# Attention with two head mixings and a routed expert layer: scores as float32 products of 64-row tiles, the second mixing in two row tiles, the split for the first mixing on GpSimd

## The chip, the cores and the metric

The kernel runs on one core of one Trainium2 chip. A time is device microseconds (us) of one execution of the whole program. Three runs of the kernel before are given; a change is judged against their median.

## What is computed

For each of 8 batches there are 12 heads, 448 queries and keys, and 64 features per head. The reference, cut to what matters here:

```
scores = (q @ k^T) / 8                              # per batch and head: 448 x 448
scores = einsum('bhij,hg->bgij', scores, w_pre)     # first mixing, over heads
attn   = softmax(scores)                            # over the keys j
attn   = einsum('bhij,hg->bgij', attn, w_post)      # second mixing, over heads
x      = attn @ v                                   # rows of 12 * 64 = 768
out    = gate * relu(x @ w1[e]) @ w2[e]             # e: the best of 8 experts for each row
```

All of it is in float32. The expert layer works on 3584 rows of x.

## The kernel before

The attention works in 32 tiles of up to 120 queries (four to a batch: 120, 120, 120 and 88). Within a tile, the head mixing goes by blocks of 10 queries, so that 10 x 12 = 120 (query, head) rows fill the partitions; the last block of a batch has 8 queries. There are 360 blocks.

- `qk` (line 196) computes the scores of one head of a tile. Both operands are kept as a rounded part and a remainder in the format float32r: the 128 contraction rows hold 64 rows of rounded q and 64 rows of its remainder, and two products, with rounded keys (line 203) and with their remainder (line 204), add up in PSUM. ScalarE copies the result to the tile `si` (line 208). The rounded parts are made by `split_k` (lines 96 and 97) and `split_q` (lines 116 and 117), on ScalarE and VectorE; keys and queries are loaded twice, once for each half of the partitions (lines 89 and 109).
- `relayout` (line 215) is a DMA on the queue of SyncE (SP) that turns 10 queries x 12 heads of `si` into a tile `sb` of 120 partitions x 448 keys.
- `split` (lines 223 and 224) makes a rounded part `sh` and a remainder `sl` of `sb`, on VectorE.
- `mix` (from line 227) is the first mixing: three float32r products of 448 columns (lines 231 to 233), the maximum of each row (line 235, VectorE), the exponential with its row sum (line 237, ScalarE), the reciprocal of the sum (lines 239 and 241), and a copy of the second mixing's weights scaled by it, `wp` (line 243, VectorE).
- `post` (from line 247) is the second mixing: four plain float32 products, one per chunk of 112 keys, each with the exponentials of the chunk as the stationary operand and the 120 columns of `wp` as the moving one (line 256). ScalarE copies the result to `pt` (line 258).
- `av` (from line 263) multiplies `pt` by the values, for a pair of heads at a time: eight float32 products in two column tiles of 64 columns (line 271). `rows` (line 289) turns x and adds the routing logits, and `dispatch` (from line 301) writes the token lists of the experts, with an indirect DMA on GpSimd (line 334).

A loop over the blocks (from line 406) hands out this work one step after another, with leads: scores 17 blocks ahead, relayout 5, split 2, the second mixing 3 behind. The code within a step is sorted by a number, but that is not the order in which the engines run it: outside the prologue (line 393) a planner orders the instructions of each engine by when it reckons their operands ready, with this order as the priority. Each engine then runs its own list strictly in order. The values of the next batch are loaded into the single tile `vt` after the last `av` of a batch (line 277), the keys of the next batch during the scores of a batch's last tile (line 210).

After the attention the expert layer follows, from about 1153 us on. It is left as it is, but for one buffer less for its raw weights and an earlier start of the first weight loads.

Of the kernel before, what the change touches and what calls it, by code (L numbers as in the profile page):

```python
# [8 lines left out]
F32 = mybir.dt.float32  # L9
# [5 lines left out]
ALU = mybir.AluOpType  # L15
# [23 lines left out]
def attn_moe_kernel(ctx, tc, qT, kT, v, w_pre, w_post, w_gate, w1, w2, out):  # L39
# [15 lines left out]
    kq = ctx.enter_context(ExitStack())  # L55
    kraw_p = kq.enter_context(tc.tile_pool(name="kraw", bufs=2, side="right"))
    k_p = kq.enter_context(tc.tile_pool(name="kp", bufs=6, side="right"))
    q_p = kq.enter_context(tc.tile_pool(name="qp", bufs=1, side="right"))
    att = ctx.enter_context(ExitStack())
    v_p = att.enter_context(tc.tile_pool(name="vp", bufs=1))  # L60
    si_p = att.enter_context(tc.tile_pool(name="sip", bufs=2))
    sb_p = att.enter_context(tc.tile_pool(name="sbp", bufs=4))
    sh_p = att.enter_context(tc.tile_pool(name="shp", bufs=3))
    e_p = att.enter_context(tc.tile_pool(name="ep", bufs=5))
    sm_p = att.enter_context(tc.tile_pool(name="smp", bufs=4))
    ps_s = att.enter_context(tc.tile_pool(name="ps_s", bufs=1, space=PSUM))
# [5 lines left out]
    bank_s = [ps_s.tile([P, 512], F32, name=f"bs{n}") for n in range(2)]  # L72
    bank_m = [ps_m.tile([IT, 512], F32, name=f"bm{n}") for n in range(2)]
    bank_p = [ps_p.tile([JC, 512], F32, name=f"bp{n}") for n in range(2)]
    bank_a = ps_a.tile([P, 3, IT], F32, name="ba")
    bank_x = [ps_x.tile([P, 512], F32, name="bx"), bank_s[0]]
    turn = {"s": 0, "m": 0, "p": 0}

    def bank(k, banks):
        turn[k] += 1  # L80
        return banks[turn[k] % len(banks)]

    KK, QQ, VV, SI, SB, SH, EE, PT, XT, KR = ({} for _ in range(10))

    def dma_k(b, c, pool):
        raw = pool.tile([P, KC, S], F32, name="kraw")
        src = kT[b, c * KC:(c + 1) * KC].rearrange("h d j -> d h j")
        for half in range(2):
            nc.sync.dma_start(out=raw[half * D:(half + 1) * D], in_=src)
        KR[b, c] = raw  # L90

    def split_k(b, c, eng=None):
        raw = KR.pop((b, c))
        ka = k_p.tile([P, KC, S], F32R, name="ka")
        kb = k_p.tile([P, KC, S], F32R, name="kb")
        nc.scalar.copy(out=ka, in_=raw)
        (eng or nc.vector).tensor_sub(out=kb, in0=raw, in1=ka.bitcast(F32))  # L97
        KK[b, c] = (ka, kb)

    def load_k(b, c):  # L100
        dma_k(b, c, kraw_p)
        split_k(b, c)

    def dma_q(T):
        b, it, ni, _ = geom[T]
        raw = q_p.tile([P, H, IT], F32, name="qraw")
        src = qT[b, :, H * it * IT:H * (it * IT + ni)].rearrange("d (h i) -> d h i", h=H)
        for half in range(2):
            nc.sync.dma_start(out=raw[half * D:(half + 1) * D, :, :ni], in_=src)
        KR[T] = raw  # L110

    def split_q(T):
        b, it, ni, _ = geom[T]
        raw = KR.pop(T)
        qs = q_p.tile([P, H, IT], F32R, name="qs", bufs=2)
        nc.scalar.copy(out=qs[:, :, :ni], in_=raw[:, :, :ni])
        nc.vector.tensor_sub(out=qs[D:P, :, :ni], in0=raw[D:P, :, :ni],
                             in1=qs[D:P, :, :ni].bitcast(F32))
        QQ[T] = qs

    def load_q(T):
        dma_q(T)
        split_q(T)

    def load_v(b):
        vt = v_p.tile([JC, NJ, HD], F32, name="vt")
        nc.sync.dma_start(out=vt, in_=v[b].rearrange("(c p) f -> p c f", p=JC))
        VV[b] = vt

    w12 = const.tile([IT, 2, H], F32, name="w12")  # L130
    for n, w in enumerate((w_pre, w_post)):
        nc.scalar.dma_start(out=w12[:, n, :], in_=w.unsqueeze(0).to_broadcast([IB, H, H]))
# [3 lines left out]
    first = ExitStack()  # L136
    first_p = first.enter_context(tc.tile_pool(name="kfirst", bufs=H // KC))
    dma_q(0)
    for c in range(H // KC):
        dma_k(0, c, first_p)  # L140

# [4 lines left out]
    # mask[p, i] = 1 where p // 12 == i  # L146
    mask = const.tile([IT, IB], F32, name="mask")
    nc.gpsimd.memset(mask, 1.0)
    nc.gpsimd.affine_select(out=mask, in_=mask, pattern=[[-H, IB]], compare_op=ALU.is_ge,
                            fill=0.0, base=0, channel_multiplier=1)  # L150
    nc.gpsimd.affine_select(out=mask, in_=mask, pattern=[[H, IB]], compare_op=ALU.is_ge,
                            fill=0.0, base=H - 1, channel_multiplier=-1)
    Wraw = const.tile([IT, IB, H], F32, name="Wraw")
    WH = const.tile([IT, IT], F32R, name="WH")
    WL = const.tile([IT, IT], F32R, name="WL")
    Wpost = const.tile([IT, H, IB], F32, name="Wpost")
    # SCALE is a power of two: exact
    nc.vector.scalar_tensor_tensor(out=Wraw, in0=w12[:, 0:1, :].to_broadcast([IT, IB, H]),
                                   scalar=SCALE, in1=mask.unsqueeze(2).to_broadcast([IT, IB, H]),
                                   op0=ALU.mult, op1=ALU.mult)  # L160
    nc.vector.tensor_tensor(out=Wpost, in0=w12[:, 1, :].unsqueeze(2).to_broadcast([IT, H, IB]),
                            in1=mask.unsqueeze(1).to_broadcast([IT, H, IB]), op=ALU.mult)
    Wraw = Wraw.rearrange("p i g -> p (i g)")
    nc.vector.tensor_copy(out=WH, in_=Wraw)
    nc.vector.tensor_sub(out=WL, in0=Wraw, in1=WH.bitcast(F32))

    # xg[:, c] = [identity | w_gate of chunk c]: rows of x and partial logits in one product
# [4 lines left out]
    tri = const.tile([P, P], BF16, name="tri")      # tri[m, n] = 1 where m < n  # L172
# [14 lines left out]
    # rows that no token has taken: a token id out of range, gate 0  # L187
# [8 lines left out]
    def qk(T, h):  # L196
        b, it, ni, _ = geom[T]
        if h == 0:
            SI[T] = si_p.tile([IT, H, S], F32, name="si")
        ps = bank("s", bank_s)  # L200
        ka, kb = KK[b, h // KC]
        qs = QQ[T][:, h, :ni]
        nc.tensor.matmul(out=ps[:ni, :S], lhsT=qs, rhs=ka[:, h % KC, :], start=True, stop=False)  # L203
        nc.tensor.matmul(out=ps[:ni, :S], lhsT=qs, rhs=kb[:, h % KC, :], start=False, stop=True)  # L204
        if T == 0 and h % 3 == 2:
            nc.vector.tensor_copy(out=SI[T][:ni, h, :], in_=ps[:ni, :S])
        else:
            nc.scalar.copy(out=SI[T][:ni, h, :], in_=ps[:ni, :S])  # L208
        if it == 3 and b + 1 < B and h % KC == KC - 1:
            load_k(b + 1, h // KC)  # L210

    def relayout(T, s):
        nb = geom[T][3][s]
        sb = sb_p.tile([IT, S], F32, name="sb")
        nc.sync.dma_start(out=sb[:nb * H], in_=SI[T][s * IB:s * IB + nb])
        SB[T, s] = sb

    def split(T, s):
        R = geom[T][3][s] * H
        sb = SB.pop((T, s))  # L220
        sh = sh_p.tile([IT, S], F32R, name="sh")
        sl = sh_p.tile([IT, S], F32R, name="sl")
        nc.vector.tensor_copy(out=sh[:R], in_=sb[:R])  # L223
        nc.vector.tensor_sub(out=sl[:R], in0=sb[:R], in1=sh[:R].bitcast(F32))  # L224
        SH[T, s] = (sh, sl)

    def mix(T, s):
        R = geom[T][3][s] * H
        sh, sl = SH.pop((T, s))
        pm = bank("m", bank_m)  # L230
        nc.tensor.matmul(out=pm[:R, :S], lhsT=WH[:R, :R], rhs=sh[:R], start=True, stop=False)  # L231
        nc.tensor.matmul(out=pm[:R, :S], lhsT=WL[:R, :R], rhs=sh[:R], start=False, stop=False)  # L232
        nc.tensor.matmul(out=pm[:R, :S], lhsT=WH[:R, :R], rhs=sl[:R], start=False, stop=True)  # L233
        st = sm_p.tile([IT, 4], F32, name="st")
        nc.vector.reduce_max(out=st[:R, 0:1], in_=pm[:R, :S], axis=AX.X, negate=True)  # L235
        et = e_p.tile([IT, S], F32, name="et")
# [8 lines left out]
        EE[T, s] = (et, wp)  # L245

    def post(T, s):
        nb = geom[T][3][s]
        R = nb * H
        if s == 0:  # L250
            PT[T] = pt_p.tile([JC, NJ, H, IT], F32, name="pt")
# [420 lines left out]
```

## Time and profile before

| what | value |
|---|---|
| runs | 1745.09, 1730.40, 1741.92 us; median 1741.92 us |
| profiled execution | span 1726.5 us from the first to the last instruction; the page gives no other time of its own |
| busy time of TensorE (matmul) | 1541.7 us, 89% of the span |
| busy time of VectorE, ScalarE, GpSimd | 1055.8, 903.9, 109.3 us |
| mean granted TensorE clock | 0.949 |
| DMA | 219.58 MB, 127 GB/s on average |

A row of the trace gives a start in us from the beginning of the span and a duration. A float32 matmul stands in it as two matmul records, each with a weight load of its own; a float32r matmul is one record. The duration of a matmul record includes the way through the array, so that records overlap: how fast TensorE works is read from the distance between starts. PE is TensorE's matmul, PEld its weight load, DVE is VectorE, ACT is ScalarE, POOL is GpSimd.

### The profile page before, as it was taken

What the parts mean: (1) busy time and instruction counts of PE and PEld (TensorE: products, weight loads), DVE (VectorE), ACT (ScalarE), POOL (GpSimd) and SP (SyncE); (2) the same over time, 40 slices, a digit from 0 to 9 for tenths busy, and PEclk for the clock granted to TensorE, in tenths of its full rate; (3) what the DMA queues carried; (4) which work ended last, traced back from release to release, by engine and by line L of the source; (5) the groups of instructions that cost most, each with busy time, mean ns of one, the idle gap of its engine ahead of it and who ended that gap; (6) DMA issues with size and microseconds to landing.
All of it is one profiled execution on the core that took longest, in us unless ns stands there. A gap on an engine that the chain in (4) does not pass through costs nothing. (4 is left out here: it accounts for less than half of the span.)

```text
span 1726.5 us, 30276 instructions
## 1 busy us (share of the span) xinstructions
PE 1541.7 (89%) x11032; PEld 1341.1 (78%) x11032; DVE 1055.8 (61%) x3159; ACT 903.9 (52%) x1940; POOL 109.3 (6%) x119
## 2 busy tenths in 40 slices
PE   5878978987988988998898898968999999999996
PEld 3667867876876877786787787758898988898986
DVE  4677857876877777786786787753433425335330
ACT  4566756765766656675775676633422314224220
POOL 1000000000000000000000000010110201101000
PEclk9999988999999989998998999988999999999998
DMA  8666656666556666665665655634514326145210
GB/s 180 129 134 129 127 117 137 116 134 140 118 126 148 121 137 128 130 126 129 134 117 128 133 110 114 154 70 162 195 67 165 142 78 215 66 153 210 74 62 34
DMA packets 112169, 219.58 MB, mean 127 GB/s; under 512 B 28226, under 2 KB 83538, under 8 KB 112004
## 3 DMA queue, kind: packets, MB, share of 16 engines
q1 hardware_dynamic: 104896, 193.53, 48.3%
q0 software_dynamic: 6064, 23.86, 3.7%
q8 instruction: 98, 1.61, 0.4%
q14 instruction: 67, 0.55, 0.1%
q10 hardware_dynamic: 1044, 0.04, 0.0%
HBM read 118.03 MB, written 23.06 MB: 82 GB/s over the span
## 5 line engine op out<-in xcount | busy, mean ns | idle before, releaser
L256 PE MATMUL bp<-wp,et 120*112 120x120 f32 (+1 forms) x2880 | 386.1, 276 | 4.2 <-ACT pt L258 2.7
L256 PEld LDWEIGHTS bp<-wp,et 120*112 120x112 f32 (+1 forms) x2880 | 346.7, 180 | 45.4 <-issue 21.4
L258 ACT COPY pt<-bp 112x480 f32<-112x480 f32 x360 | 204.3, 568 | 143.1 <-PE bp L256 142.2
L208 ACT COPY si<-bs 120x448 f32<-120x448 f32 (+1 forms) x380 | 200.8, 531 | 140.4 <-PE bs L204 108.0
L271 PE MATMUL ba<-pt,vt 112*64 112x120 f32 (+1 forms) x3072 | 210.7, 276 | 50.1 <-DMA vt<-in_v 40.7
L237 ACT ACTIVATE et<-bm,st 120x448 f32<-120x448 f32 x360 | 229.5, 638 | 43.2 <-DVE st L235 34.9
L271 PEld LDWEIGHTS ba<-pt,vt 112*64 112x64 f32 x3072 | 162.6, 142 | 110.7 <-issue 95.5
L235 DVE TENSOR_REDUCE st<-bm 120x1 f32<-120x448 f32 x360 | 220.9, 614 | 12.4 <-PE bm L233 12.1
L224 DVE TENSOR_TENSOR sl<-sb,sh 120x448 fp32r<-120x448 f32 x360 | 220.5, 615 | 0.3
L223 DVE CAST sh<-sb 120x448 fp32r<-120x448 f32 x360 | 140.0, 389 | 101.6 <-PE bm L232 51.3
L203 PE MATMUL bs<-ka,qs 128*120 128x448 f32 (+1 forms) x384 | 153.7, 400 | 48.0 <-ACT si L208 33.1
L231 PE MATMUL bm<-sh,WH 120*120 120x448 f32 x360 | 167.6, 465 | 7.6 <-DVE sh L223 4.7
L204 PE MATMUL bs<-kb,qs 128*120 128x448 f32 (+1 forms) x384 | 148.5, 387 | 0.6 <-DVE kb L97 0.6
L500 PE MATMUL pm_h<-xh,ah 128*128 128x512 f32 (+1 forms) x384 | 146.9, 383 | 2.2 <-PEq L552 0.8
L500 PE MATMUL pm_h<-xl,ah 128*128 128x512 f32 (+1 forms) x384 | 146.4, 381 | 0.0
L500 PE MATMUL pm_h<-xh,al 128*128 128x512 f32 (+1 forms) x384 | 146.4, 381 | 0.0
L233 PE MATMUL bm<-sl,WH 120*120 120x448 f32 x360 | 137.6, 382 | 0.2 <-DVE sl L224 0.2
L232 PE MATMUL bm<-sh,WL 120*120 120x448 f32 x360 | 137.5, 382 | 0.0
L519 PE MATMUL pm_y<-bh,hh 128*128 128x384 f32 x480 | 127.9, 343 | 0.0
L504 DVE SCALAR_TENSOR_TENSOR hl<-pm_h,hh 128x512 fp32r<-128x512 f32 (+1 forms) x64 | 42.0, 656 | 136.3 <-ACT hh L503 136.3
L203 PEld LDWEIGHTS bs<-ka,qs 128*120 128x120 f32 (+1 forms) x384 | 72.6, 189 | 67.0 <-ACT si L208 39.9
L519 PE MATMUL pm_y<-bl,hh 128*128 128x384 f32 x480 | 123.6, 336 | 0.0
(106 smaller groups left out, 2177.4 us busy)
## 6 DMA issues: line engine op xcount, KB each, us to landing
sb<-si SPq DMA_DIRECT2D x352, 210.0 KB
wraw<-in_w SPq DMA_DIRECT2D x48, 512.0 KB
wraw<-in_w SPq DMA_DIRECT2D x64, 384.0 KB
kraw<-in_kT SPq DMA_DIRECT2D x96, 224.0 KB
qraw<-in_qT SPq DMA_DIRECT2D x48, 360.0 KB
vt<-in_v SPq DMA_DIRECT2D x8, 1344.0 KB
XD<-xr SPq DMA_DIRECT2D x24, 360.0 KB
qraw<-in_qT SPq DMA_DIRECT2D x16, 264.0 KB
```

What stands on the lines that cost most here:

```text
L203: nc.tensor.matmul(out=ps[:ni, :S], lhsT=qs, rhs=ka[:, h % KC, :], start=True, stop=False)
L204: nc.tensor.matmul(out=ps[:ni, :S], lhsT=qs, rhs=kb[:, h % KC, :], start=False, stop=True)
L208: nc.scalar.copy(out=SI[T][:ni, h, :], in_=ps[:ni, :S])
L224: nc.vector.tensor_sub(out=sl[:R], in0=sb[:R], in1=sh[:R].bitcast(F32))
L231: nc.tensor.matmul(out=pm[:R, :S], lhsT=WH[:R, :R], rhs=sh[:R], start=True, stop=False)
L235: nc.vector.reduce_max(out=st[:R, 0:1], in_=pm[:R, :S], axis=AX.X, negate=True)
L237: nc.scalar.activation(out=et[:R], in_=pm[:R, :S], func=AF.Exp, bias=st[:R, 0:1], scale=1.0, accum_out=st[:R, 1:2])
L256: nc.tensor.matmul(out=ppv[:, c, :], lhsT=et[:R, c * JC:(c + 1) * JC], rhs=wp[:R, :, :nb], start=True, stop=True)
L258: nc.scalar.copy(out=PT[T][:, :, :, s * IB:s * IB + nb].rearrange("p c h i -> p (c h) i"), in_=pp[:, :NJ * R].rearrange("p (x i) -> p x i" ...
L271: nc.tensor.matmul(out=pa[r * D:(r + 1) * D, :ni], lhsT=VV[b][:, c, h * D:(h + 1) * D], rhs=PT[T][:, c, h, :ni], start=(c == 0), stop=(c = ...
L500: nc.tensor.matmul(out=ph[:, :n], lhsT=wx[:, fs], rhs=xx[:, kt, :n], start=(m == 0), stop=(m == 3 * NK1 - 1))
L519: nc.tensor.matmul(out=py[g][:, :384], lhsT=hx[:, kt, ts], rhs=wx[:, g * 384:(g + 1) * 384], start=(n == 0), stop=(n == 3 * NK2 - 1))
```

## The change

- The scores are plain float32 products. A pair of heads lies in one tile of 128 partitions (64 each), and the two heads are multiplied in two row tiles of the array, each over 224 keys at a time, into two PSUM banks. ScalarE copies both banks in one instruction. Keys and queries are no longer split, and are loaded once. There are buffers for the keys of two batches.
- A step now holds two blocks of 10 queries, side by side in the free dimension (`[P, 2, S]`), so there are 184 steps. The 120 rows lie on partitions 4 to 123, so that the first five queries end at partition 64.
- The first mixing keeps its three float32r products per block. The rounded part and the remainder are made by GpSimd, for both blocks in one instruction each, as is the scaled `wp`.
- The second mixing runs in two row tiles: five queries in partitions 4 to 63, five in 64 to 123. Each product has 60 columns in place of 120, and each row tile has a PSUM bank of its own. VectorE copies the results, one instruction per bank.
- The values have two tiles, and those of the next batch are loaded at step 8 of a batch. The leads are, in steps of two blocks: scores 9, relayout 3, split 1; the second mixing is 1 behind.

```
 def qk(T, c):
...
+        for n in range(2):
+            ns = slice(n * S // 2, (n + 1) * S // 2)
+            for r in range(2):
+                hs = slice(r * D, (r + 1) * D)
+                nc.tensor.matmul(out=bank_s[:ni, r, ns], lhsT=qt[hs, c, :ni], rhs=kt[hs, ns],
+                                 start=True, stop=True)
+        nc.scalar.copy(out=SI[T][:ni, 2 * c:2 * c + 2, :], in_=bank_s[:ni, :, :S])
+        if it == 1 and b + 1 < B:
+            load_k(b + 1, c)
...
 def relayout(T, s):
+        sb = sbs[nsb["n"] % len(sbs)]
+        nsb["n"] += 1
+        for c, nq in enumerate(geom[T][3][s]):
+            q0 = s * NB + c * IB
+            nc.sync.dma_start(out=sb[R0:R0 + nq * H, c, :], in_=SI[T][q0:q0 + nq])
...
 def split(T, s):
-        nc.vector.tensor_copy(out=sh[:R], in_=sb[:R])
-        nc.vector.tensor_sub(out=sl[:R], in0=sb[:R], in1=sh[:R].bitcast(F32))
+        sh = sh_p.tile([P, 2, S], F32R, name="sh")
+        sl = sh_p.tile([P, 2, S], F32R, name="sl")
+        nc.gpsimd.tensor_copy(out=sh[:R1, :nh], in_=sb[:R1, :nh])
+        nc.gpsimd.tensor_sub(out=sl[:R1, :nh], in0=sb[:R1, :nh], in1=sh[:R1, :nh].bitcast(F32))
...
 def mix(T, s):
+        for c in range(nh):
+            for n, (w, x) in enumerate(((WH, sh), (WL, sh), (WH, sl))):
+                nc.tensor.matmul(out=bank_m[:R1, c, :S], lhsT=w[:R1, :], rhs=x[:R1, c, :],
+                                 start=(n == 0), stop=(n == 2))
+        nc.vector.reduce_max(out=st[:R1, 0, :nh], in_=bank_m[:R1, :nh, :S], axis=AX.X, negate=True)
+        for c in range(nh):
+            nc.scalar.activation(out=et[:R1, c, :], in_=bank_m[:R1, c, :S], func=AF.Exp,
+                                 bias=st[:R1, 0, c:c + 1], scale=1.0,
+                                 accum_out=st[:R1, 1, c:c + 1])
...
+        wp = e_p.tile([P, 2, WPC], F32, name="wp")
+        for c in range(nh):
+            nc.gpsimd.tensor_scalar(out=wp[:R1, c, :], in0=Wpost[:R1], scalar1=st[:R1, 2, c:c + 1],
+                                    scalar2=None, op0=ALU.mult)
...
 def post(T, s):
+        for n in range(len(halves)):
+            for c in range(NJ):
+
+                for r in range(2):
+                    ps = slice(64 * r, 64 if r == 0 else R1)
+                    x0 = (n * NJ + c) * WPC
+                    nc.tensor.matmul(out=bank_p[r][:, x0:x0 + WPC],
+                                     lhsT=et[ps, n, c * JC:(c + 1) * JC],
+                                     rhs=wp[ps, n, :], start=True, stop=True)
+        for r in range(2):
+            pv = bank_p[r][:, :2 * NJ * WPC].rearrange("p (n x i) -> p n x i", n=2, i=IQ)
+            if len(halves) == 2:
...
+                nc.vector.tensor_copy(out=dst, in_=pv.rearrange("p n x i -> p x n i"))
...
 def av(T, pr):
-        if pr == NPAIR - 1 and it == 3 and b + 1 < B:
-            load_v(b + 1)
...
-    PL, QLEAD, RLEAD, SLEAD = 3, 17, 5, 2
+    PL, QLEAD, RLEAD = 1, 9, 3
...
+            at(max(u0 - QLEAD - 3, -1), 0, load_q, T)
+        if it == 0 and b + 1 < B:
+            at(u0 + 8, 2, load_v, b + 1)
+        for c in range(NPAIR):
+            at(max(u0 - QLEAD + c * 5 // 6, -1), 3, qk, T, c)
         for s in range(n):
             at(max(u0 + s - RLEAD, -1), 4, relayout, T, s)
-            at(max(u0 + s - SLEAD, -1), 5, split, T, s)
+            at(max(u0 + s - 1, -1), 5, split, T, s)
             at(u0 + s, 1, mix, T, s)
             at(u0 + s + PL, 7, post, T, s)
...
-            wpool["raw"] = moe.enter_context(tc.tile_pool(name="wrp", bufs=4, side="right"))
+            wpool["raw"] = moe.enter_context(tc.tile_pool(name="wrp", bufs=3, side="right"))
...
-        if u > ustart[NTILE - 1] and u - ustart[NTILE - 1] <= NK1:
-            load_w(0, w1, u - ustart[NTILE - 1] - 1, FF, "a")
+        if u > ustart[NTILE - 1] - 3 and u - ustart[NTILE - 1] + 3 <= NK1:
+            load_w(0, w1, u - ustart[NTILE - 1] + 2, FF, "a")
```

## Rows read from the trace of the kernel before

**Rows 1.** The page: busy time by engine, and in 40 slices of the span (about 43 us each) TensorE's busy share and the granted clock, in tenths.

```profile
PE 1541.7 (89%) x11032; PEld 1341.1 (78%) x11032; DVE 1055.8 (61%) x3159; ACT 903.9 (52%) x1940; POOL 109.3 (6%) x119
PE   5878978987988988998898898968999999999996
PEclk9999988999999989998998999988999999999998
```

**Rows 2.** Three stretches of the attention at full clock, with TensorE's instructions of line 231 alone, one per block of 10 queries: the stretch, its length, their busy time and count, granted clock, DMA share, GB/s.

```profile
145.00:214.00 69.00, 12.05 (x27) 1.00 0.61 123
...
705.00:775.00 70.00, 12.50 (x28) 1.00 0.60 120
...
985.00:1050.00 65.00, 11.16 (x25) 1.00 0.59 117
```

**Rows 3.** TensorE in order of time: the first product of the first mixing, and the last second mixing.

```profile
31.91 0.73 PE L231 MATMUL bm<-sh,WH 120*120 120x448 f32 x1
...
1142.23 0.94 PE L256 MATMUL bp<-wp,et 96*112 96x96 f32 x8
```

**Rows 4.** TensorE's longest waits in the attention, over the whole run: engine, output and line, what was waited for, us in total, how often, the longest.

```profile
PE ba L271 <- DMA vt<-in_v: 40.7, 7, 6.8
PE bs L203 <- ACT si L208: 33.1, 14, 5.6
PE bx L289 <- DVE xt L275: 28.3, 7, 5.6
```

**Rows 5.** One stretch after such a wait: us, then busy time and count of PE, PEld, DVE, ACT and POOL, granted clock, DMA share, GB/s.

```profile
218.70:229.00 10.30, 7.39 (x44) 5.77 (x44) 3.48 (x16) 1.73 (x4) 0.99 (x1) 0.50 0.43 114
```

**Rows 6.** TensorE in order of time in a full-clock stretch: start, us from the first to the last end of the merged records, line, tiles, rows*columns of the stationary operand, shape of the moving one, count.

```profile
511.64 0.98 PE L256 MATMUL bp<-wp,et 120*112 120x120 f32 x8
512.39 0.44 PE L231 MATMUL bm<-sh,WH 120*120 120x448 f32 x1
512.67 0.37 PE L232 MATMUL bm<-sh,WL 120*120 120x448 f32 x1
512.88 0.37 PE L233 MATMUL bm<-sl,WH 120*120 120x448 f32 x1
513.08 0.36 PE L203 MATMUL bs<-ka,qs 128*120 128x448 f32 x1
513.28 0.37 PE L204 MATMUL bs<-kb,qs 128*120 128x448 f32 x1
513.58 1.04 PE L271 MATMUL ba<-pt,vt 112*64 112x120 f32 x16
514.55 1.07 PE L256 MATMUL bp<-wp,et 120*112 120x120 f32 x8
515.39 0.44 PE L231 MATMUL bm<-sh,WH 120*120 120x448 f32 x1
515.67 0.36 PE L232 MATMUL bm<-sh,WL 120*120 120x448 f32 x1
```

**Rows 7.** The weight loads (PEld) of the same stretch, in order of time.

```profile
512.36 0.18 PEld L231 LDWEIGHTS bm<-sh,WH 120*120 120x120 f32 x1
512.47 0.18 PEld L232 LDWEIGHTS bm<-sh,WL 120*120 120x120 f32 x1
```

**Rows 8.** Groups by line and shape: count, busy time and mean ns of one, idle time of the engine before them and what ended it.

```profile
L237 ACT ACTIVATE et<-bm,st 120x448 f32<-120x448 f32 x352 | 224.5, 638 | 43.1 <-DVE st L235 34.9 <-DVE lgs L305 2.9 <-DVE st L241 1.2
L235 DVE TENSOR_REDUCE st<-bm 120x1 f32<-120x448 f32 x352 | 216.0, 614 | 12.2 <-PE bm L233 11.9
L224 DVE TENSOR_TENSOR sl<-sb,sh 120x448 fp32r<-120x448 f32 x352 | 215.6, 615 | 0.3
L208 ACT COPY si<-bs 120x448 f32<-120x448 f32 x284 | 150.4, 534 | 122.2 <-PE bs L204 92.2 <-DMA sb<-si 13.3 <-issue 8.9
L237 ACT ACTIVATION_READ_ACCUMULATOR et<-bm,st 120x1 f32 x352 | 69.7, 198 | 0.0
L241 DVE RECIPROCAL st<-st 120x1 f32<-120x1 f32 x352 | 55.1, 157 | 3.4
L239 DVE TENSOR_SCALAR st<-st 120x1 f32<-120x1 f32 x352 | 52.3, 149 | 53.4 <-ACT et L237 47.8 <-issue 2.3
L206 DVE COPY si<-bs 120x448 f32<-120x448 f32 x4 | 2.5, 622 | 3.0 <-PE bs L204 3.0
```

**Rows 9.** The same view, GpSimd alone: its indirect DMA of the dispatch, and its elementwise instructions with one input.

```profile
L334 POOL DMA_INDIRECT TB<-tg,di x32 | 33.5, 1047 | 1116.1 <-DVE wp L243 814.3 <-DVE di L333 294.1 <-DVE nslot L472 7.6
L171 POOL COPY xg<-ident 128x128 f32<-128x128 f32 x6 | 1.5, 283 | 0.0
L149 POOL TENSOR_SCALAR_AFFINE_SELECT mask<-mask 120x10 f32<-120x10 f32 x1 | 0.2, 187 | 0.0
```

**Rows 10.** VectorE in order of time, in the stretch of rows 6.

```profile
511.53 0.61 DVE L235 TENSOR_REDUCE st<-bm 120x1 f32<-120x448 f32 x1
512.07 0.61 DVE L224 TENSOR_TENSOR sl<-sb,sh 120x448 fp32r<-120x448 f32 x1
513.04 0.15 DVE L239 TENSOR_SCALAR st<-st 120x1 f32<-120x1 f32 x1 [0.35 <-ACT et L237]
```

More of the change, by code (lines that the diff above doesn't have):

```diff
@@ L77, in attn_moe_kernel @@
[L77 to L87, printed above, removed]
-        for half in range(2):
[L89 to L119, printed above, removed]
@@ L121, in load_q, with load_k @@
-    def load_q(T):
-        dma_q(T)
-        split_q(T)
+    bank_x = [ps_x.tile([P, 512], F32, name="bx"), bank_s[:, 0, :]]
+    KK, QQ, VV, SI, SB, SH, EE, PT, XT = ({} for _ in range(9))
+    def load_k(b, c):
+        kt = k_p.tile([P, S], F32, name="kt")
+        nc.sync.dma_start(out=kt, in_=kT[b, 2 * c:2 * c + 2].rearrange("h d j -> (h d) j"))
+        KK[b, c] = kt
+    def load_q(T):
+        b, it, ni, _ = geom[T]
+        qt = q_p.tile([P, NPAIR, IT], F32, name="qt")
+        src = qT[b, :, H * it * IT:H * (it * IT + ni)].rearrange("d (c t i) -> t d c i", c=NPAIR, t=2)
+        for half in range(2):
+            nc.sync.dma_start(out=qt[half * D:(half + 1) * D, :, :ni], in_=src[half])
+        QQ[T] = qt
@@ L135, in attn_moe_kernel @@
     nc.scalar.activation(out=warm, in_=warm, func=AF.Exp)
[L136 to L140, printed above, removed]
+    load_q(0)
+    for c in range(NPAIR):
+        load_k(0, c)
     ident = const.tile([P, P], F32, name="ident")
     make_identity(nc, ident)
-    mask = const.tile([IT, IB], F32, name="mask")
+    mask = const.tile([P, IB], F32, name="mask")
     nc.gpsimd.memset(mask, 1.0)
@@ new lines, in attn_moe_kernel @@
+    WH = const.tile([P, R1], F32R, name="WH")
+    WL = const.tile([P, R1], F32R, name="WL")
+    nc.vector.tensor_copy(out=WH, in_=Wpre)
+    nc.vector.tensor_sub(out=WL, in0=Wpre, in1=WH.bitcast(F32))
+    nc.vector.tensor_tensor(out=Wpost, in0=w12[:, 1, :].unsqueeze(2).to_broadcast([P, H, IQ]),
+                            in1=mask5.unsqueeze(1).to_broadcast([P, H, IQ]), op=ALU.mult)
+    Wpost = Wpost.rearrange("p g i -> p (g i)")
+    sbs = [sb_p.tile([P, 2, S], F32, name=f"sb{n}") for n in range(3)]
@@ L193, in attn_moe_kernel, with qk @@
                         in_=none.unsqueeze(1).to_broadcast([P, 8, ROWS // P // 8, 2]))
-    def qk(T, h):
+    def qk(T, c):
         b, it, ni, _ = geom[T]
-        if h == 0:
+        if c == 0:
             SI[T] = si_p.tile([IT, H, S], F32, name="si")
[L200 to L210, printed above, removed]
```

130 lines of the change are left out of this document (55 added, 75 removed).

## The prediction

> **What bounds the kernel now.** I read the page first: TensorE is busy 89% of the span, and its slices stay at 8 or 9 through attention and experts, with the granted clock dipping only in the attention [rows 1]. The expert layer is hardly touched, so the question is the attention, from 31.91 us, the first product of a first mixing, to about 1143 us, the last second mixing [rows 3]: 1111 us for 360 blocks, 3.09 us each. Next I counted blocks in stretches without stalls. There 80 blocks take 204 us, 2.55 us each [rows 2], so 5.10 us for two blocks, which is a step of the changed kernel. 360 x 2.55 = 918 us; the other 193 us of the attention are stalls and half clock.
>
> The 5.10 us are TensorE's own, as the order of time shows [rows 6]. Float32r products of 448 columns start 0.205 us apart (512.67, 512.88, 513.08, 513.28). The eight records of a second mixing run from 511.64 to 512.465 (the second product of the next mixing, 512.67, less 0.205): 0.103 us a record, 0.82 a block. A pair of `av` takes from 513.49 to 514.64 (515.67 less 0.205 less 0.82): 1.15 us. Its 16 records have the same 120 moving columns, so one after another they would need 1.65: the two column tiles run side by side, in 8 x 0.103 = 0.82, and 0.33 go to entering and leaving the tiles. Two blocks: mixing 6 x 0.205 = 1.23, scores 4 x 0.205 = 0.82, second mixing 1.64, one `av` pair 1.15; with a tile's `rows` spread over its steps, some 0.25, that is 5.09. TensorE is full there, and faster helpers gain nothing there.
>
> The 193 us are the other half of the picture. TensorE waits 40.7 us for the values of the next batch, seven times, 33.1 for score copies and 28.3 for x [rows 4]. The last two come at batch ends, where ScalarE and VectorE split new keys and queries. 102.1 us together; after such a wait the granted clock is 0.50 for some us, 10.3 in one place [rows 5]. The rest is half clock, the first tile and short waits.
>
> **The change, part by part.**
>
> *Waits removed.* Values with two tiles, loaded at step 8 of the batch before, have some 15 steps to land, so the 40.7 us go. Keys and queries are loaded once and not split, so what blocked ScalarE and VectorE at batch ends goes too. With these waits their half clock goes. The transfers stay on SP's queue behind the relayouts; bytes per step fall, so I charge nothing, and if values delay a relayout, its lead of three steps (16 us) covers it. I keep 30 of the 193 us: the first tile, the last tile, and chance.
>
> *Scores.* Records of 224 columns by the 0.103 us of 120: 0.19 us. A pair of heads has four matmuls, eight records, two abreast as in `av`: 4 x 0.19 = 0.76 instead of 0.82 for two heads. If the pairs are offset by one record it is five slots, 0.95. I take 0.76, as `av` fills eight slots with 16 records: -0.06.
>
> *Second mixing.* Sixty moving columns would halve the stream: 16 records in 16 slots for two blocks, 0.052 each, 0.84 in place of 1.64. But each record still needs its load of 112 columns. Two loads into the same rows stood 0.11 us apart for 120 columns (512.36, 512.47) [rows 7]; scaled, 0.10 for 112. So a slot is 0.10 and the block pair takes 1.61. Bounds: 0.84, if a load of half the rows takes half, and 3.2, if the tiles load in turn. I take 1.61: -0.03.
>
> The Trainium skill, "TensorE: Matmul & The Clock Gate", section "LDWEIGHTS (loading the stationary operand)", says that a load's time goes by columns alone, not rows, at columns / 1.2 ns: 93 ns for 112 columns as an estimate, which speaks against any gain here and gives the same sum as 0.10; no row shows a 64-row load.
>
> *Entering and leaving tiles.* The 0.33 us around an `av` pair are two changes, 0.17 each [rows 6]. In the order of a step (mixing, scores, `av`, second mixing) there are now four, about 0.18 each as most first loads have 112 or 120 columns, not 64: 0.72, so +0.39. If scores and second mixing stand together it is three: +0.2.
>
> *First mixing.* Same products per block; 124 rows in place of 120 cost nothing on TensorE, where columns count. One pair of banks in place of two: the next mixing waits for the first exponential. That is the maximum, at most 2 x 0.614, and 0.638 [rows 8], 1.9 us; scores, `av` and second mixing with their changes last over 3.5 between two mixings. Hidden.
>
> *Other engines, per step.* VectorE: maximum 1.23, sum and reciprocal 0.31, two copies to `pt` at 0.622 x 480/448 = 0.67 each [rows 8]; 2.9, some 3.6 with x and dispatch. It loses the split of two blocks (2 x 0.615 for the remainder alone). ScalarE: 2 x (0.638 + 0.198) and a score copy of at most 2 x 0.534: 2.7. Both fit under 5.4 with room.
>
> *GpSimd* is new in the loop. One-input instructions take 0.187 us for 10 elements and 0.283 for 128 [rows 9]: 0.18 fixed and 0.81 ns an element. The copy of 896 elements: 0.91. No row has two inputs; bounds for copy and remainder together: 1.82 (the second input costs nothing) and 5.94 (no fixed part: 2.21 ns an element from the copy's 283 ns for 128, and twice that with two inputs). I take twice the slope, 1.64, since the two-length rows do show a fixed part: 2.55 together. With two `wp` (0.23 each) and a sixth of 1.047 for the dispatch: 3.2 us a step. It fits too.
>
> The Trainium skill, "GPSIMD Engine Reference", section "Engine selection", speaks against this move: two-input elementwise work belongs on VectorE, GpSimd being about twice as slow. Its figure of 4497 ns for 2048 elements makes 1.97 us here, an estimate, and 3.5 us a step; no row shows it, and the sum would not change.
>
> *A new wait in a queue.* `wp` on GpSimd waits for the reciprocal, and whatever stands behind it waits along: the split of the next step, and on it the next mixing. If the split stands in front, it runs a step ahead and hides. VectorE's list shows how the planner does this: the remainder for a later block (512.07) stands between the maximum (511.53) and the sum (513.04) [rows 10], though the code has it behind. I expect the same on GpSimd.
>
> *The rest.* The raw weights' third buffer in place of four: TensorE is full in the expert slices [rows 1], which hides it; at 0 to +10 us. Earlier start: no key split before the first scores; -5 us.
>
> *Sum.* Step: 5.10 - 0.06 - 0.03 + 0.39 = 5.40 us. Attention: 180 x 5.40 + 30 = 1002 against 1111, -109; with the start -114. The span becomes 1726.5 - 114 = 1612. The runs shown lie 3.9 to 18.6 us above the profiled span, their median 15.4: 1612 + 15 = 1627, and I say **1625 us**. With the step between 5.2 and 5.75 (all costs at their ends) 1590 to 1690.
>
> **The rivals.**
>
> *A, row tiles take turns (slower).* If loads of the two row tiles don't overlap, second mixing needs 32 x 0.10 = 3.2 and scores 8 x 0.105 = 0.84: +1.67 a step, +300, **1925 us**; if the products too go in turn, scores are 1.52: 2050. It is slower from +0.65 a step on. For it: no row has row tiles. Against: `av`'s column tiles do run abreast, loads included.
>
> *B, GpSimd becomes the bound.* From 4.76 us for copy and remainder on it sets the step; from 5.4 nothing is gained; at 5.94 a step is 6.58 and the time 1842. For it: the two-input price is unmeasured. Against: the fixed part in rows 9.
>
> *C, the split stands behind `wp`.* Then products (1.0), maximum (1.2), two exponentials (1.5), sum and reciprocal (0.4), two `wp` (0.5), split (2.55) and semaphores follow one another: 7.5 us a step, 2.1 more, **2010 us**. Against: rows 10.
>
> *D, stalls stay.* New waits at the tile ends, or half clock, keep 100 of the 193 us: 1695.
>
> *E, weight loads of 60 to 64 rows are quick.* Second mixing 0.84: -0.77 a step, **1485 us**. Against: rows 7, if rows don't count.
>
> **How the numbers follow.** Forecast 0.56, D 0.14, E 0.06, B 0.10 (a fifth of it still faster), A 0.08, C 0.06. A change under 1% can't be told from none. Faster: 0.56 + 0.14 + 0.06 + 0.02 = 0.78. Same: 0.02, from B's middle. Slower: 0.06 + 0.08 + 0.06 = 0.20. The range 1550 to 1745 holds the forecast with its bounds, D, and the near half of B: 0.75 to 0.8.
>
> **What would show it.** Right: no wait for `vt`, granted clock near 1.00 through the attention, score records in pairs 0.19 us apart, second-mixing records in pairs 0.10 apart, GpSimd busy about 3.2 us per 5.4. Wrong: starts of the two row tiles 0.1 apart instead of together (A); GpSimd busy over 90% (B); GpSimd's `wp` ahead of the split, and the first mixing waiting for it (C); slots of 0.052 in the second mixing (E).

## The result, and the profile after

The changed kernel takes 1671.03 us (median of four runs, 1664.03 to 1676.02) against 1739.24 for the kernel before: a ratio of 0.960, with a 95% interval of 0.955 to 0.965. The forecast was 1625, in a range of 1550 to 1745. The profiled span fell from 1726.5 to 1662.0 us, where the prediction's sum said 1612. Four executions of the experiments below ran slow (three of e1's ten, at 1754.67 to 1760.82 us, and one of e4's five, at 3198.11 us), and the times and ratios given leave them out.

The page of the changed kernel: busy time by engine, and in 40 slices TensorE's busy share and the granted clock.

```profile
PE 1554.0 (94%) x14680; PEld 1336.8 (80%) x14680; DVE 838.5 (50%) x1838; ACT 618.2 (37%) x1312; POOL 813.1 (49%) x850
PE   5999999998999999999999997959999999999996
PEclk9999989998999999999999997779999999999998
```

Against [rows 1], VectorE and ScalarE lost 217 and 286 us of work and GpSimd gained 704; TensorE's busy share in the attention's slices rose from mostly 8 and 9 to 9 in nearly all.

Blocks counted in stretches at full clock, as in [rows 2]. Line 224 holds all three products of a block, so a block has three records.

```profile
240.00:360.00 120.00, 33.18 (x135) 1.00 0.60 122
...
490.00:625.00 135.00, 37.37 (x152) 1.00 0.60 120
...
780.00:1005.00 225.00, 61.32 (x248) 1.00 0.57 107
```

That is 535 records, 178.3 blocks, in 480 us: 2.69 us a block, 5.38 for a step. Before it was 5.10, so a step without stalls is slower by 0.28 us, about as forecast (5.40). TensorE in order of time shows where it goes, as in [rows 6].

```profile
300.74 0.37 PE L224 MATMUL bm<-sl,WH 124*124 124x448 f32 x1
301.04 1.02 PE L190 MATMUL bs<-kt,qt 64*120 64x224 f32 x8
301.99 1.43 PE L278 MATMUL ba<-pt,vt 112*64 112x88 f32 x32
303.35 1.78 PE L252 MATMUL bp<-wp,et 64*112 64x60 f32 x32
305.06 0.22 PE L321 MATMUL bx<-ohb,tri 120*120 120x8 bf16 x1
...
305.45 0.36 PE L224 MATMUL bm<-sh,WL 124*124 124x448 f32 x1
```

From the end of one mixing, 300.74 + 0.205 = 300.945, to the start of the next, 305.45 - 0.205 = 305.245, there are 4.30 us. The eight score records end within 1.04 us, changes of tiling included; one after another they would need 8 x 0.19 = 1.52. So they run in pairs: unmerged, the starts of a pair lie 0.007 us apart and the pairs 0.189. The 32 records of the second mixing also run in pairs, 0.098 us apart, where 60 columns alone would need 0.052 (half of the 0.103 for 120). Their weight loads of 112 columns are as far apart, so it is the load that sets the pace. With 0.76 for the scores, 16 x 0.076 = 1.22 for two `av` pairs of 88 columns, 1.57 for the second mixing and some 0.1 for two small products, about 0.65 us remain for four changes of tiling (e5 prices one directly).

TensorE's waits in the attention, as in [rows 4].

```profile
PE bs L190 <- ACT si L192: 33.1, 25, 6.7
PE bm L224 <- ACT et L228: 14.0, 11, 7.1
```

The 40.7 us for values and the 28.3 for x are gone. The wait for score copies is as long as before over the whole run; 8.0 us of it lie ahead of the first mixing and 25.1 behind. The next rows show why it stayed: SP's queue, ScalarE and TensorE around the longest of these waits. In a row of SP's queue (SPq) the time is that of issuing the transfer, not of its landing.

```profile
367.49 3.37 SPq L205 DMA_DIRECT2D sb<-si  x2
370.95 2.65 SPq L89 DMA_DIRECT2D kt<-in_kT  x1
373.70 2.36 SPq L301 DMA_DIRECT2D XD<-xr  x1
378.39 0.91 ACT L192 COPY si<-bs 120x896 f32<-120x896 f32 x1 [6.13 <-DMA sb<-si]
379.35 1.85 PE L190 MATMUL bs<-kt,qt 64*120 64x224 f32 x8 [6.71 <-ACT si L192]
```

The copy of a new tile's scores waits 6.13 us for a relayout, not for scores. There are two buffers `si`; the third tile's scores go into the first one's, whose last relayout was issued by 370.86 (367.49 + 3.37), with keys and rows of x issued right behind it. The copy starts at 378.39, some 7.5 us later. TensorE waits behind the copy for 6.71 us, and then runs at half clock (granted 0.50 from 379 to 386 us; the records of 379.35 take 1.85 us, those of 301.04 1.02).

### The profile page after: what moved, and what is told of

It is laid out like the page before. It is cut to its first block, busy times and chain, and to the rows that moved or that the text cites. A ratio compares the mean times of both kernels' runs of the same rounds, so it can differ in the third digit from the quotient of the medians.

```text
span 1662.0 us, 36295 instructions
## 1 busy us (share of the span) xinstructions
PE 1554.0 (94%) x14680; PEld 1336.8 (80%) x14680; DVE 838.5 (50%) x1838; ACT 618.2 (37%) x1312; POOL 813.1 (49%) x850
## 5 line engine op out<-in xcount | busy, mean ns | idle before, releaser
L214 POOL TENSOR_TENSOR sl<-sb,sh 124x896 fp32r<-124x896 f32 (+1 forms) x184 | 377.0, 2049 | 15.7
L228 ACT ACTIVATE et<-bm,st 124x448 f32<-124x448 f32 x360 | 224.9, 630 | 399.2 <-DVE st L226 277.0
L252 PEld LDWEIGHTS bp<-wp,et 60*112 60x112 f32 (+1 forms) x5760 | 323.3, 179 | 28.5 <-issue 15.5
L252 PE MATMUL bp<-wp,et 60*112 60x60 f32 (+1 forms) x5760 | 340.7, 264 | 3.3 <-POOL wp L236 3.3
L260 DVE COPY pt<-bp 112x480 f32<-112x480 f32 x352 | 216.0, 651 | 131.6 <-PE bp L252 129.8
L213 POOL CAST sh<-sb 124x896 fp32r<-124x896 f32 (+1 forms) x184 | 168.9, 918 | 227.9 <-PE bm L224 185.0
L190 PE MATMUL bs<-kt,qt 64*120 64x224 f32 (+1 forms) x1536 | 220.7, 396 | 40.0 <-ACT si L192 33.1
L226 DVE TENSOR_REDUCE st<-bm 124x2 f32<-124x896 f32 (+1 forms) x184 | 196.7, 1069 | 92.9 <-PE bm L224 88.7
L192 ACT COPY si<-bs 120x896 f32<-120x896 f32 (+1 forms) x192 | 173.0, 901 | 111.0 <-PE bs L190 79.2
L224 PE MATMUL bm<-sh,WH 124*124 124x448 f32 x360 | 155.2, 431 | 16.9 <-ACT et L228 14.0
```

The costliest lines, as they stand in the source:

```text
L190: nc.tensor.matmul(out=bank_s[:ni, r, ns], lhsT=qt[hs, c, :ni], rhs=kt[hs, ns], start=True, stop=True)
L192: nc.scalar.copy(out=SI[T][:ni, 2 * c:2 * c + 2, :], in_=bank_s[:ni, :, :S])
L213: nc.gpsimd.tensor_copy(out=sh[:R1, :nh], in_=sb[:R1, :nh])
L214: nc.gpsimd.tensor_sub(out=sl[:R1, :nh], in0=sb[:R1, :nh], in1=sh[:R1, :nh].bitcast(F32))
L224: nc.tensor.matmul(out=bank_m[:R1, c, :S], lhsT=w[:R1, :], rhs=x[:R1, c, :], start=(n == 0), stop=(n == 2))
L226: nc.vector.reduce_max(out=st[:R1, 0, :nh], in_=bank_m[:R1, :nh, :S], axis=AX.X, negate=True)
```

## The experiments

All times stand beside runs of the kernel before on the same chip, 1740.72 us for e1 to e4, 1748.18 for e5 to e8, 1745.58 for e9 and e10. The ratios are those on record with the runs; they differ from the quotients of the medians by up to 0.3%. The three groups ran on three chips, so a difference between runs of two groups is given by ratios or profiled spans too.

**e1, one tile for the values.** Of the forecast's parts this is the largest that can be undone alone.

```
-    v_p = [kq.enter_context(tc.tile_pool(name="vp0", bufs=1, side="right")),
-           att.enter_context(tc.tile_pool(name="vp1", bufs=1))]
+    v_p = att.enter_context(tc.tile_pool(name="vp", bufs=1))
...
+        if pr == NPAIR - 1 and it == 3 and b + 1 < B:
+            load_v(b + 1)
...
-        if it == 0 and b + 1 < B:
-            at(u0 + 8, 2, load_v, b + 1)
```

> The changed kernel with one tile for the values again, loaded after the last product of a batch. If the changed kernel's gain comes from the wait for the values, seven waits of about 6 us come back, and some 10 us of half clock behind each: 41 + 35 us, so 1730 to 1750 us, level with the kernel before. If the gain comes from the lighter ScalarE and VectorE at batch ends, it stays under 1690.

Measured: 1734.19 us, ratio 0.999 (0.994 to 1.003). The whole gain is gone, as expected for this cause. TensorE's longest wait is the old one, and longer, 9.1 us each time in place of 5.8.

```profile
PE ba L277 <- DMA vt<-in_v: 63.5, 7, 10.3
```

So with one tile for the values, row tiles, the split on GpSimd, unsplit keys and the lighter engines together bring nothing over the kernel before; taken away last, the second tile is worth the whole 4%. That is a net: the waits for x are gone in e1 too, but each step is longer (by 0.28 us, as shown above), and each wait for values is. The reverse was not tried, a second tile for values in the kernel before, so it stays open how much of the 4% it would have brought there without the rest.

**e2, the first expert's weights later.**

```
-        if u > ustart[NTILE - 1] - 3 and u - ustart[NTILE - 1] + 3 <= NK1:
-            load_w(0, w1, u - ustart[NTILE - 1] + 2, FF, "a")
+        if u > ustart[NTILE - 1] and u - ustart[NTILE - 1] <= NK1:
+            load_w(0, w1, u - ustart[NTILE - 1] - 1, FF, "a")
```

> The changed kernel with the first expert's raw weights loaded from where the kernel before loads them. Theory: the early casts of these weights stand on ScalarE in front of exponentials and wait for their transfer, which costs TensorE 7.1 and 3.0 us and the half clock behind them: 20 to 35 us faster than 1671. Rival: the weights then come late for the first expert, and the time stays within 8 us.

Measured: 1672.51 us, ratio 0.962 (0.958 to 0.966): no change. The stall in front of an exponential is still there, 6.8 us long, in the last tile; only its place moved, so its price was not measured. The time is the rival's, but not its reason: the expert layer, from its first transpose to the end, took 564.8 us (565.9 in the changed kernel), so the weights did not come late for it.

**e3, the scores one step later.**

```
-    PL, QLEAD, RLEAD = 1, 9, 3
+    PL, QLEAD, RLEAD = 1, 8, 3
```

> The changed kernel with the scores 8 steps ahead in place of 9. Theory: score copies wait for a buffer that the last relayouts of the tile before last still read, and one step of slack removes this: ScalarE's 20 us of waits for sb<-si go, TensorE's 33 us for score copies fall to under 10, and the time falls by 15 to 30 us from 1671. Rival: the wait only moves to the relayout behind the scores, and the time stays within 8 us.

Measured: 1629.62 us, ratio 0.939 (0.934 to 0.943), some 40 us below the changed kernel (41 by the medians, 38 by the profiled spans of 1662.0 and 1624.2), more than expected. ScalarE's score copies in the changed kernel, then in e3; then TensorE's wait in e3.

```profile
L192 ACT COPY si<-bs 120x896 f32<-120x896 f32 (+1 forms) x192 | 173.0, 901 | 111.0 <-PE bs L190 79.2 <-DMA sb<-si 20.1 <-issue 8.8
```

```profile
L192 ACT COPY si<-bs 120x896 f32<-120x896 f32 (+1 forms) x192 | 173.0, 901 | 70.2 <-PE bs L190 70.2
```

```profile
PE bs L190 <- ACT si L192: 17.1, 29, 1.0
```

The 20.1 us for `sb<-si` are gone, TensorE's wait is halved and no single one is over 1.0 us; the mean granted clock rises from 0.959 to 0.975. Over the whole run TensorE's wait did not fall under 10 us, as I had written: 8.0 us of it lie ahead of the first mixing, and 9.1 of the 25.1 behind it are left. What remains is the copy of one score pair before the next, since both use the same two banks. One number in the schedule had held back 38 us of the 50 by which my sum was off, both by profiled spans. (It also moves the loads of queries by a step.)

The rival's wait did come: with scores a step later, relayouts are later, and GpSimd's split waits 121.1 us for them in e3 where it waited 35.4. In this kernel it costs little: TensorE's wait for `wp`, which stands behind the split, rises from 3.3 to 10.6 us. e9 shows what it costs elsewhere.

**e4, the split on ScalarE and VectorE.**

```
-        nc.gpsimd.tensor_copy(out=sh[:R1, :nh], in_=sb[:R1, :nh])
-        nc.gpsimd.tensor_sub(out=sl[:R1, :nh], in0=sb[:R1, :nh], in1=sh[:R1, :nh].bitcast(F32))
+        nc.scalar.copy(out=sh[:R1, :nh], in_=sb[:R1, :nh])
+        nc.vector.tensor_sub(out=sl[:R1, :nh], in0=sb[:R1, :nh], in1=sh[:R1, :nh].bitcast(F32))
```

> The changed kernel with the rounded part made by ScalarE and the remainder by VectorE, as wp stays on GpSimd. Theory: TensorE sets the pace and the engine of the split does not matter: within 1% of 1671. On VectorE the scalings that wait out GpSimd's remainder fall back, L231 from 337 to about 150 ns and L318 from 1217 to about 225. Rival 1: GpSimd's hold on VectorE costs time: 20 us faster or more. Rival 2: VectorE needed the relief: 20 us slower or more.

Measured: 1677.56 us, ratio 0.966 (0.961 to 0.971): within 1%. The two scalings behaved as expected. Their rows in the changed kernel, then in e4, with the remainder on VectorE.

```profile
L231 DVE TENSOR_SCALAR st<-st 124x2 f32<-124x2 f32 x176 | 59.3, 337 | 154.3 <-ACT et L228 153.9 <-issue 0.3
L318 DVE TENSOR_SCALAR ohb<-iota,sc 120x8 bf16<-120x8 f32 x24 | 29.2, 1217 | 0.1
```

```profile
L214 DVE TENSOR_TENSOR sl<-sb,sh 124x896 fp32r<-124x896 f32 x176 | 190.5, 1082 | 41.3 <-ACT sh L213 40.6
L231 DVE TENSOR_SCALAR st<-st 124x2 f32<-124x2 f32 x176 | 29.6, 168 | 53.1 <-ACT et L228 48.1
L318 DVE TENSOR_SCALAR ohb<-iota,sc 120x8 bf16<-120x8 f32 x24 | 5.4, 225 | 0.0
```

The verdict holds for scores 9 steps ahead, where the split seldom waits for its relayout, as ScalarE's row in e4 says:

```profile
ACT sh L213 <- DMA sb<-si: 31.7, 12, 4.3
```

e9 repeats the experiment with scores 8 steps ahead.

**e5, scores beside the second mixing** (on e3).

```
-            at(max(u0 - QLEAD + c * 5 // 6, -1), 3, qk, T, c)
+            at(max(u0 - QLEAD + c * 5 // 6, -1), 3 if u0 - QLEAD + c * 5 // 6 < 0 else 6.5, qk, T, c)
```

> On e3 (scores 8 steps ahead, 1630 us): the scores of a step stand behind av and in front of the second mixing, both in row tiles, so that a step changes the array's tiling three times in place of four. Theory: one change is about 0.15 us and is paid in some 150 of the 184 steps: 20 to 25 us faster than e3. Rival: changes cost nothing that other waits would not fill, and the time stays within 8 us of e3.

Measured: 1655.69 us, ratio 0.947 (0.945 to 0.950), slower than e3 by 15 us (by the ratios) to 26 (by the medians). Neither case came: steps without a wait are shorter, but a new wait takes more than they give. First one step in e3, then the same step in e5, from the first product of a mixing to that of the next:

```profile
249.15 0.45 PE L224 MATMUL bm<-sh,WH 124*124 124x448 f32 x1
...
254.18 0.47 PE L224 MATMUL bm<-sh,WH 124*124 124x448 f32 x1
```

```profile
256.86 0.45 PE L224 MATMUL bm<-sh,WH 124*124 124x448 f32 x1
...
261.72 0.47 PE L224 MATMUL bm<-sh,WH 124*124 124x448 f32 x1
```

That is 5.03 us against 4.86. Seven different steps of a batch, compared in the same way, are 0.17 to 0.19 us shorter in e5, so one change of tiling costs about that much. The new wait is TensorE's longest in e5's attention; behind it, GpSimd ahead of one instance.

```profile
PE bp L252 <- POOL wp L236: 28.7, 16, 3.4
```

```profile
472.28 0.93 POOL L213 CAST sh<-sb 124x896 fp32r<-124x896 f32 x1 [5.21 <-DMA sb<-si]
473.30 2.07 POOL L214 TENSOR_TENSOR sl<-sb,sh 124x896 fp32r<-124x896 f32 x1
475.55 1.05 POOL L339 DMA_INDIRECT TB<-tg,di  x1 [0.18 <-issue]
476.65 0.85 POOL L236 TENSOR_SCALAR wp<-Wpost,st 124x60 f32<-124x60 f32 x2
477.15 3.24 PE L252 MATMUL bp<-wp,et 64*112 64x60 f32 x31 [3.37 <-POOL wp L236]
```

The scores come later within the step, so the relayout does, and GpSimd stands 5.21 us on it with `wp` queued behind. In sum the split waits for relayouts as long as in e3 (123.5 us against 121.1), but after the first one seven of these waits are over 4.6 us long, against two in e3.

**e6, the second mixing without row tiles** (on e3).

```
-WPC = H * IQ
+WPC = H * IB
...
-                for r in range(2):
-                    ps = slice(64 * r, 64 if r == 0 else R1)
-                    x0 = (n * NJ + c) * WPC
-                    nc.tensor.matmul(out=bank_p[r][:, x0:x0 + WPC],
-                                     lhsT=et[ps, n, c * JC:(c + 1) * JC],
-                                     rhs=wp[ps, n, :], start=True, stop=True)
+                nc.tensor.matmul(out=bank_p[n][:, c * WPC:(c + 1) * WPC],
+                                 lhsT=et[:R1, n, c * JC:(c + 1) * JC],
+                                 rhs=wp[:R1, n, :], start=True, stop=True)
...
```

> On e3: the second mixing without row tiles, four products of 120 columns per block over all 124 rows, as in the kernel before, and wp of 120 columns on GpSimd. Theory: weight loads of 112 columns set the row tiles' slots (0.098 us against 0.103 for 120 columns), so that the row tiles gain 0.08 us a step and cost one change of tiling, 0.15: e6 is 0 to 20 us faster than e3. Rival: the row tiles halve the second mixing, and undoing them costs 0.8 us in 180 steps: 100 us slower or more.

Measured: 1629.16 us, ratio 0.933 (0.931 to 0.936): as fast as e3, or a little faster. The rival, that row tiles halve the second mixing, is out by 100 us.

**e7, the weights behind the attention** (on e3).

```
-        if u > ustart[NTILE - 1] - 3 and u - ustart[NTILE - 1] + 3 <= NK1:
-            load_w(0, w1, u - ustart[NTILE - 1] + 2, FF, "a")
+        if NU < u <= NU + NK1:
+            load_w(0, w1, u - NU - 1, FF, "a")
```

> On e3: the first expert's weight loads and casts stand behind the attention in the program. Theory: ScalarE's casts no longer wait for raw weights in front of the last tile's work, the stall of 6.5 us in e3's last tile and its half clock go, and the casts fit into the 12.6 us for which TensorE waits for gathered rows: 5 to 12 us faster than e3. Rival: the first expert then waits for its weights, and the time stays or grows by up to 10 us.

Measured: 1633.71 us, ratio 0.936 (0.933 to 0.939): not to be told from e3. The stall stayed, 6.9 us. In e7's last tile:

```profile
1004.24 1.04 ACT L359 CAST ah<-wraw 128x1024 fp32r<-128x1024 f32 x1 [8.02 <-DMA wraw<-in_w]
1005.32 1.23 DVE L360 TENSOR_TENSOR al<-wraw,ah 128x1024 fp32r<-128x1024 f32 x1 [7.53 <-ACT ah L359]
...
1007.46 0.52 DVE L282 COPY xt<-ba 128x360 f32<-128x360 f32 x1
1008.04 1.72 PE L294 MATMUL bx<-xg,xt 128*120 128x136 f32 x6 [6.88 <-DVE xt L282]
```

The cast still stands in the last tile, although it is behind the attention in the program: the planner puts it where it reckons the weights to have landed. The theory of the cause stands in these rows (cast, remainder, copy of x, each behind the other in its queue), but the edit did not remove it, so its price was not measured.

**e8, a fourth buffer for raw weights, and the first copies shared** (on e3).

```
+        if T == 0:
+            nc.scalar.copy(out=SI[T][:ni, 2 * c, :], in_=bank_s[:ni, 0, :S])
+            nc.vector.tensor_copy(out=SI[T][:ni, 2 * c + 1, :], in_=bank_s[:ni, 1, :S])
...
+    wpool["raw"] = moe.enter_context(tc.tile_pool(name="wrq", bufs=4))
```

> On e3, two parts in stretches of their own: four buffers for raw weights in the expert layer, and the first tile's score copies shared by ScalarE and VectorE, one bank each. Theory: the expert layer, from its first transpose to the end, falls from 565 to 559 us, as in the kernel before; the first product of a first mixing comes at 27 to 30 us in place of 33.0. Together 6 to 12 us faster than e3. Rival: three buffers cost nothing and the 6 us come from elsewhere; the expert layer stays at 564 to 566.

Measured: 1634.69 us, ratio 0.937 (0.933 to 0.941): no change. The expert layer, from its first transpose to the end, took 561.6 us (559.0 before the change, 565.9 after, 564.7 in e3). The first mixing began later, not earlier, at 34.8 us: it waits for GpSimd's first split, and that for the first relayout, issued when the first tile's copies are done. Sharing the copies did not speed them: VectorE's began only when ScalarE's had ended, and the score pairs came 3.14 us apart in place of 2.86.

**e9, e4's edit on e3.** With the wait for score buffers gone, the question of e4 again. e9 differs from e4 in the lead of the scores alone.

> On e3 (0.9385 of the kernel before): the split on ScalarE and VectorE as in e4, now without the wait for score buffers. Theory: TensorE sets the pace, so the engine of the split does not matter: ratio 0.93 to 0.945. Rival 1: GpSimd's hold on VectorE and the second mixing's waits for wp (10.6 us in e3) cost time, and without them it is 0.92 or less. Rival 2: with TensorE undisturbed, the copies and exponentials on ScalarE and VectorE now queue behind the split: 0.95 or more.

Measured: 1725.01 us, ratio 0.989 (0.986 to 0.993), some 90 us slower than e3 (95 by the medians, 86 by the profiled spans) and far past rival 2's bound. It is also some 40 us slower than e4 (ratio 0.966): the lead that gains 40 us with the split on GpSimd loses as much with it on ScalarE. One instance in e9, on ScalarE and TensorE:

```profile
303.05 0.94 ACT L213 CAST sh<-sb 124x896 fp32r<-124x896 f32 x1 [4.80 <-DMA sb<-si]
303.89 0.90 ACT L192 COPY si<-bs 120x896 f32<-120x896 f32 x1
...
304.85 1.67 PE L190 MATMUL bs<-kt,qt 64*120 64x224 f32 x8 [2.59 <-ACT si L192]
```

ScalarE is busy only 46% of the span, so it isn't the work. The split waits 4.80 us for its relayout, and the score copy queues behind it, with TensorE waiting. So rival 2's queue is the cause, but what stands in it is a wait for a transfer. In sum, in e9, to set beside the 31.7 us of e4:

```profile
PE bs L190 <- ACT si L192: 71.5, 39, 4.9
...
ACT sh L213 <- DMA sb<-si: 120.5, 39, 5.7
```

In e3 GpSimd waits nearly as long for the same transfers (121.1 us, 24.0 of them before its first split), and nobody stands behind it on the way to TensorE but `wp`. First e3's split on GpSimd, then TensorE's wait for `wp` there.

```profile
L213 POOL CAST sh<-sb 124x896 fp32r<-124x896 f32 (+1 forms) x184 | 169.0, 918 | 215.4 <-DMA sb<-si 121.1 <-PE bm L224 87.2 <-PE bp L252 6.7
```

```profile
PE bp L252 <- POOL wp L236: 10.6, 11, 2.1
```

**e10, e6 and the fourth buffer together** (on e3; the two edits are shown above).

> On e3: the second mixing without row tiles (e6) and four buffers for raw weights in the expert layer (the part of e8 that shortened it, from 564.7 to 561.6 us). Expected: 0 to 10 us faster than e3, ratio 0.928 to 0.938; faster than the kernel before and than the changed one. If the expert layer is back at 565, the buffers were not what shortened it.

Measured: 1626.22 us, ratio 0.933 (0.929 to 0.936): faster than the kernel before by 6.7%, as expected, and not to be told from e6. The expert layer took 568.7 us, so the fourth buffer was not what shortened it in e8.

## Why the prediction was right, point by point

The sign, the mechanism and the range were right; the size was 117 us forecast and 68 measured. One of the signs to look for did not come: the clock was not near 1.00 through the attention, as the stalls that stayed bring half clock with them. By the profiled spans the miss is 1662 - 1612 = 50 us.

- **TensorE is full outside stalls, and the gain is in the waits.** Right. The step went from 5.10 to 5.38 (forecast 5.40), a loss, and e1 shows that without the second value tile nothing is gained. That the waits for x went with the key splits fits the rows, but no run puts the splits back.
- **Scores in pairs, 0.76.** Right, pairs 0.189 us apart. **Second mixing 1.61 a step.** Right, 1.57, and e6 confirms that row tiles gain nothing there. Loads of 112 columns and 60 or 64 rows stand 0.098 us apart in each row tile, against 0.11 for 120 columns and 120 rows in [rows 7]. The Trainium skill's rule ("TensorE: Matmul & The Clock Gate", section "LDWEIGHTS (loading the stationary operand)"), that a load's time goes by columns and not by rows, fits this; its 93 ns for 112 columns is an estimate somewhat under the 98 measured. Rivals A and E fall with these rows.
- **Changes of tiling, 0.72 a step.** Right in size: about 0.65 in the step shown, and e5 gives 0.17 to 0.19 for one. One change less shortens the step; e5 as a whole got slower by another wait.
- **Waits removed, 30 us kept of 193.** This is the step that failed. The attention from the first mixing (33.35 us) to the end of the last second mixing (1074.23) took 1040.9 us; 180 x 5.38 = 968 of it are steps, so 72 stayed where I had kept 30: over half of the way to rival D's 100. I had argued that a relayout delayed by other loads is covered by its lead of three steps. That lead covers the split, which reads what the relayout writes. It does not cover the score copy, which overwrites what the relayout reads: scores 9 steps ahead refill a buffer whose last relayout is issued one step earlier, or in the same step where the tile of 88 queries, with five steps, lies between. e3 moves the scores by a step, and the attention takes 1005.2 us, near the 1002 of the sum. The term was mis-sized by this wait.
- **GpSimd, 3.2 us a step.** Too low, without effect. Its rows, for [rows 9]:

```profile
L214 POOL TENSOR_TENSOR sl<-sb,sh 124x896 fp32r<-124x896 f32 x176 | 368.0, 2091 | 15.0
L213 POOL CAST sh<-sb 124x896 fp32r<-124x896 f32 x176 | 164.2, 933 | 220.3 <-PE bm L224 177.4 <-DMA sb<-si 35.4 <-PE bs L190 3.7
L236 POOL TENSOR_SCALAR wp<-Wpost,st 124x60 f32<-124x60 f32 x360 | 153.5, 438 | 84.4 <-DVE st L233 80.1 <-issue 2.0 <-DMA sb<-si 1.3
```

  The copy was right (0.93 for 0.91). The remainder takes 2.09, not 1.64, and `wp` 0.44, not 0.23: 4.1 us a step, still under 5.38, so B did not come. The Trainium skill's figure ("GPSIMD Engine Reference", section "Elementwise — side-by-side cycle accounting") made 1.97 of the remainder as an estimate and was nearer than my doubled slope. The Trainium skill's section "Engine selection" on that page would leave such work on VectorE; the trace agrees on the price (1082 ns there in e4, about half). e4 and e9 don't test that advice alone, as they put the copy on ScalarE; both parts on VectorE were not run.
- **The split ahead of `wp`.** Right: GpSimd runs the split a step ahead. At 301.09 the split for a later step starts as soon as a mixing has freed its buffer; `wp` of that mixing follows at 304.71, and the next mixing at 305.17 does not wait. C did not come.

```profile
301.09 0.93 POOL L213 CAST sh<-sb 124x896 fp32r<-124x896 f32 x1
302.11 2.09 POOL L214 TENSOR_TENSOR sl<-sb,sh 124x896 fp32r<-124x896 f32 x1
304.71 0.84 POOL L236 TENSOR_SCALAR wp<-Wpost,st 124x60 f32<-124x60 f32 x2 [0.52 <-DVE st L233]
```

- **Start, -5 us.** Wrong by 6: the first mixing came at 33.35 us, where it had been 31.91 and I expected 27. Each first score pair waits for the copy of the one before (2.86 us from pair to pair), so the first relayouts are issued at 23.75 us, only 2.2 us earlier than before the change (25.97); and the first split starts 8.6 us after that, where it had been 5.5. A step's relayout is two transfers now; whether that is the reason, no run shows.
- **The rest, 0 to +10 us.** From the last second mixing to the end it is 587.7 us in place of 583.3, inside the bound though not at the 0 I took. Its cause stays open: the expert layer alone varied between 561.6 and 572.1 us over e3, e5 to e8 and e10, with nothing changed in it but the buffers of e8 and e10 and the place of its first weight loads in e7.

In sum, 39 us of the miss are the attention, 6 the start and 4 the end.

## What to carry to other kernels

When a tile buffer is refilled some steps ahead, check its refill against the last reader of its old content, transfer time included: a lead that is one step too long cost some 40 us here, while the same lead looked like slack. A shorter lead moves the wait to the reader of the transfer, so it pays only where nothing urgent stands behind that reader: place an instruction that waits for a transfer on an engine whose queue holds nothing that the bounding engine needs soon (e3 against e9), whatever the engine's busy share. And a row tile with short moving operands gains nothing when the weight load, which goes by its columns, is as long as the product it replaces.

## What the runs showed of the hardware that was not expected

GpSimd holds up some of VectorE's instructions. The scaling of a 120 x 8 tile took 1217 ns on average with the remainder on GpSimd, and 225 ns with it on VectorE (e4), as before the change; in the changed kernel one began at 302.78 and ended with GpSimd's remainder.

```profile
302.78 1.44 DVE L318 TENSOR_SCALAR ohb<-iota,sc 120x8 bf16<-120x8 f32 x1
```

Maxima and copies out of PSUM were not held: they took 1089 and 651 ns with the remainder on GpSimd, 1090 and 651 without it (e4). The Trainium skill, "GPSIMD Engine Reference", section "Specifications", says that GpSimd shares SBUF interfaces with VectorE and that VectorE instructions in a 2-port mode or with two SBUF inputs collide with it. For two SBUF inputs the rows fit it: a product of two small SBUF tiles that takes 161 ns in e4 ended with GpSimd's copy, beside which it began. Whether the scalings run in a 2-port mode, no row tells.

```profile
207.86 0.93 POOL L213 CAST sh<-sb 124x896 fp32r<-124x896 f32 x1 [1.45 <-PE bm L224]
207.86 0.95 DVE L335 TENSOR_TENSOR pos<-pos,ohb 88x8 f32<-88x8 f32 x1
```

Here the delays cost nothing that could be measured (e4); VectorE was busy 50% of the span.
